# Output-weight preparation moved ahead beside the feature-map folding, its stores issued later, and the last block's quotients multiplied on VectorE

## The chip, the cores and the metric

One core of one Trainium2 chip runs the whole kernel. The metric is the device time of one execution in microseconds (us), as a median over several runs. The work is done by TensorE (PE; its weight loads are shown as PEld), VectorE (DVE), ScalarE (ACT) and GpSimd (POOL), and SyncE (SP) issues nearly all transfers from one queue, in order.

## What is computed

```python
x  = A_x                                   # 1 x 2048 x 640
xn = layernorm(x)                          # over the 640 columns
# A: linear attention, 32 heads of 20, with a learned feature map w_phi per head
q, k, v = xn_A @ wqkv                      # 640 -> 3 * 640
phi(u)  = concat(softmax(u @ w_phi), softmax(-(u @ w_phi)))        # u = q or k, 40 features
kv, z   = phi(k)^T v, sum_s phi(k)
a = ((phi(q) kv) / (phi(q) z + 1e-6)) @ wo                         # 640 -> 640
# B: MLP, 640 -> 1728 -> 640
b = gelu(layernorm(xn) @ w1 + b1) @ w2 + b2
return x + a + b
```

`phi`'s products are folded into the weights: `wk` and `wq` are multiplied by `w_phi` once, so that keys and queries come out of one product as feature maps.

## The kernel before

All products run in float32r, with each operand split into a high and a low part (`hi`: a ScalarE copy with rounding, `lo`: the difference, one subtraction), and three matmuls per product (`mm3`, lines 70 to 72: hi by hi, hi by lo, lo by hi). The 2048 tokens are four blocks `b` of 512. The MLP's 14 chunks of 128 hidden units go in pairs `g`: `passes(g, b, ws)` makes the first layer of two chunks (PSUM bank, gelu on ScalarE at line 285, split at lines 61 and 64 into tiles `m`), and then the second layer, five banks of 128 outputs, each added by VectorE to `acc[b]` (lines 328 and 330). Three PSUM banks serve the second layer in turn, so TensorE can start a bank only when VectorE has read the one three before it.

Other work is laid beside the matmuls by hand. `Mlp.tick` is called after every group of three matmuls and advances the generator in `mlp.beside` by one step; whatever the generator emits stands at that place in each engine's program. TensorE's order is the written one throughout, and in the MLP and in the last parts of the kernel so are those of VectorE, ScalarE and GpSimd. An engine does its program in order, so an instruction that waits holds up all behind it; but an engine that waits for nobody runs ahead of the tick at which an instruction was written. SyncE's queue is ordered by a scheduler.

The places that matter here:

- `next_y`, beside pass (1, 0): y of block 1 is made from `acc1` and broadcast rows `m5`, for five chunks `c`: GpSimd subtracts (line 637), VectorE multiplies (639), ScalarE rounds (641), VectorE subtracts (643). The next pass's first matmuls read it.
- `prep`, beside the passes for blocks 0 and 1, from pass (1, 1) on. First seven jobs fold `w_phi` into `wk` and `wq` (`prep_fold`, matmuls at line 698, splits at 713 and 715). Then a list `events` of steps with tick numbers: the y of blocks 2 and 3, chunk by chunk (`load`, `centred` 769, `scaled` 772, `hi` 776, `lo` 780, and differences of them, `combine` 792 and `combined_lo` 797, stored to `y_dram` and `t_dram` from a tile `t` with two buffers), and among them `wo_steps(q)`, the output weights: load, four sums of quarter tiles on GpSimd (`add`, 817), `hi` on ScalarE (823), `lo` on GpSimd (827) with the store of both parts right behind it (829). The five chunks of `wo` make three groups `q`.
- `Attention.quotients`, for each block: after the denominators' round trip through memory, five shuffles on VectorE (1287) and five multiplications on GpSimd (1289) make `ob`.
- The output product at the end, for blocks 0 and 1 and then 2 and 3: `ob` is split (`plain`, line 1302) and combined (`combine`, 1475), the combinations are split (`turn`, 1302), and the banks are read by VectorE into the sum (1516). `plain` gives the `lo` of block 2 to GpSimd and that of the others to VectorE.

Of the kernel before, what the change touches and what calls it, by code (L numbers as in the profile page):

```python
# [8 lines left out]
F32 = mybir.dt.float32  # L9
F32R = mybir.dt.float32r  # L10
AF = mybir.ActivationFunctionType
ALU = mybir.AluOpType
# [3 lines left out]
P = 128  # L16
S, D, F, H, DH = 2048, 640, 1728, 32, 20
KC = D // P
# [28 lines left out]
def f(ap):  # L47
    return ap.bitcast(F32)
# [3 lines left out]
def tile_kernel(ctx: ExitStack, tc: tile.TileContext, x, xT, wkT, wqT, wv, wphi, wo, w1, b1, w2, b2,  # L52
                ident, mmask, emask, vsel, out):
    nc = tc.nc
# [35 lines left out]
    wo_dram = [tc.dram_tile([P, 2, 2048], F32, name=f"wo{p}") for p in "hl"]  # L90
    wo4_dram = [tc.dram_tile([P, D], F32, name=f"wo4{p}") for p in "hl"]
# [26 lines left out]
    rp = ys.enter_context(tc.tile_pool(name="raw", bufs=1))  # L118
    wp = ys.enter_context(tc.tile_pool(name="w", bufs=1))

    def mtile(i, dtype=F32):
        return mp.tile([P, 2, D if i < 5 else 512], dtype, name=f"m{i}")
    y = {}

    def load_x(ts, xp, tag="xb"):
        xbs = []
# [88 lines left out]
    class Mlp:  # L215
# [21 lines left out]
        def fetch(self, c, pool=None):  # L237

            for p in self.fetch_parts(c, pool):
                p()  # L240
# [275 lines left out]
    mlp = Mlp((0, 1, 2, 3), ((0, 2), (1, 3)))  # L516
# [51 lines left out]
    def step(gen, n):  # L568
        for _ in range(n):
            next(gen, None)  # L570
# [169 lines left out]
    def prep():  # L740
        jobs = [units[o:o + 2] for o in range(0, 14, 2)]
        ahead = raws(jobs[0])
        more = more_stats()
        for i, job in enumerate(jobs):
            for k, _ in enumerate(prep_fold(job, ahead)):
                if k == 0 and i < 6:
                    ahead = raws(jobs[i + 1])
                if i > 0 and k % 3 == 1:
                    next(more, None)
                yield  # L750

        for _ in more:
            yield
        mr = {2: load_rows(2), 3: load_rows(3, 6)}

        raw = fp.tile([P, D], F32, name="raw").rearrange("p (c d) -> p c d", c=KC)
        nc.sync.dma_start(raw, wv[:, VF * H:].rearrange("(c p) d -> p c d", p=P))
        for _ in range(8):
            yield
        split(*[w[:, :, C2:C3] for w in wkv_], raw)  # L760

        xs, hls, events = {}, {}, []

        def load(c, b):
            xs[c, b] = fp.tile([P, 512], F32, name="xq", bufs=4)
            nc.sync.dma_start(xs[c, b], xT[c * P:(c + 1) * P, b * 512:(b + 1) * 512])

        def centred(c, b):
            nc.gpsimd.tensor_tensor(xs[c, b], xs[c, b], mr[b][:, 0], op=ALU.subtract)  # L769

        def scaled(c, b):
            nc.vector.tensor_tensor(xs[c, b], xs[c, b], mr[b][:, 1], op=ALU.mult)

        def hi(*at):
            hls[at] = fp.tile([P, 2, KC, G5], F32R, name="t").rearrange("p a c f -> p a (c f)")[:, :, :512]
            nc.scalar.activation(hls[at][:, 0], xs[at], AF.Copy)

        def lo(*at):
            hl = hls.pop(at)
            nc.vector.tensor_tensor(hl[:, 1], xs[at], f(hl[:, 0]), op=ALU.subtract)  # L780
            for p in range(2):
                nc.sync.dma_start(y_dram[at[1] - 2][p][:, at[0], :], f(hl[:, p]))

        def combined(q, i):

            c0, c1 = 2 * q, 2 * q + 1
            return {0: ((c0, 2), (c0, 3), (c0, 2)), 2: ((c0, 3), (c1, 3), (c0, 3)),
                    1: ((c1, 3), (c1, 3), (c0, 2)), 3: ((c1, 2), (c1, 2), (c1, 3))}[i]

        def combine(q, i):  # L790
            out, x0, x1 = (xs[at] for at in combined(q, i))
            nc.gpsimd.tensor_tensor(out, x0, x1, op=ALU.subtract)

        def combined_lo(q, i):
            at = combined(q, i)[0]
            hl = hls.pop(at)
            nc.vector.tensor_tensor(hl[:, 1], xs[at], f(hl[:, 0]), op=ALU.subtract)
            nc.sync.dma_start(t_dram[q][:, i], f(hl))

        def wo_steps(q):  # L800

            chunks = range(2 * q, min(2 * q + 2, KC))
            raw = []

            def fetch():
                for c in chunks:
                    raw.append(fp.tile([P, D], F32, name="raw"))
                    nc.sync.dma_start(raw[-1], wo[c * P:(c + 1) * P, :])

            def add(i):  # L810
                if i == 0:
                    raw.append(rp.tile([P, 6 * P], F32, name="s"))
                sm = raw[2].rearrange("p (i k n) -> p i k n", i=3, k=2)
                (a11, a21), (a12, a22) = ([r[:, :512].rearrange("p (k j n) -> p j k n", k=2, j=2)[:, j] for j in range(2)] for r in raw[:2])
                o, x0, x1, op = ((sm[:, 0], a21, a22, ALU.add), (a21, a11, a21, ALU.subtract),
                                 (sm[:, 1], sm[:, 0], a11, ALU.subtract), (sm[:, 2], a12, sm[:, 1], ALU.subtract))[i]
                nc.gpsimd.tensor_tensor(o, x0, x1, op=op)  # L817

            his = {}

            def hi(n, o, w):
                his[n, o] = fp.tile([P, D], F32R, name="wpt", bufs=1)[:, :w]
                nc.scalar.activation(his[n, o], raw[n][:, o:o + w], AF.Copy)

            def lo(n, o, w):
                src = raw[n][:, o:o + w]
                nc.gpsimd.tensor_tensor(src.bitcast(F32R), src, f(his[n, o]), op=ALU.subtract)
                for p, x in enumerate((f(his[n, o]), src)):
                    nc.sync.dma_start(wo_dram[p][:, q, D * n + o:D * n + o + w] if q < 2 else wo4_dram[p], x)

            steps = [(0, fetch, ())]
            if q < 2:
                steps += [(10 + 2 * i, add, (i,)) for i in range(4)]
            for n, piece in enumerate([(0, 0, D), (1, 0, D), (2, 0, 384), (2, 384, 384)] if q < 2 else [(0, 0, D)]):
                steps += [(18 + 7 * n, hi, piece), (19 + 7 * n, lo, piece)]
            return steps

        for q in range(3):
            events += [(4 + 46 * q + after, 1000 + len(events), step, args) for after, step, args in wo_steps(q)]
        base = 8  # L840
        for q in range(3):
            tiles = [(c, b) for c in range(2 * q, min(2 * q + 2, KC)) for b in range(2, 4)]
            for n, at in enumerate(tiles):
                for after, step in ((-6, load), (0, centred), (3, scaled), (5, hi), (7, lo)):
                    events.append((base + 5 * n + after, len(events), step, at))
            base += 5 * len(tiles) + 5
            if q < 2:
                for n, i in enumerate((0, 2, 1, 3)):
                    for after, step in ((0, combine), (3, lambda q, i: hi(*combined(q, i)[0])), (5, combined_lo)):
                        events.append((base + 4 * n + after, len(events), step, (q, i)))  # L850
                base += 19
        tick = 0
        for at, _, step, args in sorted(events, key=lambda e: e[:2]):
            while tick < at:
                tick += 1
                yield
            step(*args)

    def load_v():

        raws = [fp.tile([P, 2, KC, G5], F32, name="t").rearrange("p a c f -> p (a c f)") for _ in range(2)]
        raws = [raw[:, o:o + VF * H] for raw in raws for o in (0, VF * H)] + [fp.tile([P, D], F32, name="raw")[:, :VF * H]]
        for kc, raw in enumerate(raws):
            nc.sync.dma_start(raw, wv[kc * P:(kc + 1) * P, :VF * H])
        return raws
# [6 lines left out]

    p01 = mlp.passes(0, 1, [wc[0], wc[1]])
    next(p01)
    mlp.beside = prep()
    p11 = mlp.passes(1, 1, [wc[2], wc[3]])
    next(p11)
    finish(p01)
# [307 lines left out]
    class Attention:  # L1186
# [72 lines left out]
        def quotients(self):  # L1259
# [25 lines left out]
            for c in range(KC + 1):  # L1285
                if c < KC:
                    nc.vector.stream_shuffle(rx[:, c, :], rx[:, c, :], SPREAD)
                if c:
                    nc.gpsimd.tensor_tensor(ob[:, c - 1, :], ob[:, c - 1, :], rx[:, c - 1, :], op=ALU.mult)
                    if self.b < 2:  # L1290
                        nc.sync.dma_start(ob_dram[self.b][:, c - 1], ob[:, c - 1])
                for i in range(3):
                    yield
# [41 lines left out]
    def first_split():  # L1335
        at[0].oh, at[0].ol = (yp.tile([P, KC, 512], F32R, name=f"y{p}0") for p in range(2))
        for c in range(KC + 1):
# [3 lines left out]
                at[0].split(c - 1, 1)  # L1341
            if c % 2:
                yield

    def both(*gens):
        for _ in zip_longest(*gens):
            yield

    wol, phs = [], []
    ep = rx = None  # L1350
# [114 lines left out]
        return [z[:, 2 * q + i] for z in (at[b0 + j].oh, at[b0 + j].ol)]  # L1465

    def plain(b, c, part):
        return lambda: at[b].split(c, part, eng=nc.gpsimd if b == 2 else nc.vector)

    def combine(b0, i, q):  # L1470

# [166 lines left out]
```

## Time and profile before

| | |
|---|---|
| median of 3 runs | 721.48 us (721.33 to 729.02) |
| profiled execution | 720.63 us, span 718.8 us |
| busy: PE, PEld, DVE | 701.6, 586.2, 530.3 us |
| busy: ACT, POOL | 353.9, 476.7 us |
| moved by DMA | 109.72 MB, mean 153 GB/s |
| granted TensorE clock | 1.0 |

The span is what the profiler sees from the first to the last instruction; the profiled execution's own time is 1.8 us longer. Tables by stage give, for each engine, busy us and the number of instructions in a stretch of the span, then clock, DMA share and GB/s. In the timeline a row is start, duration, engine, line and operation, and in brackets how long the engine stood idle before it and on whom it waited.

### The profile page before, as it was taken

To read this page: it belongs to the slowest core of one execution; us is meant where nothing else is said; L and a number is where in the kernel's file an instruction comes from. 1 tells how busy PE (TensorE), PEld (TensorE's weight loads), DVE (VectorE), ACT (ScalarE), POOL (GpSimd) and SP (SyncE) were. 2 spreads that over 40 slices of the span, in tenths; PEclk is the share of its full clock that TensorE was granted. 3 is DMA by queue.
4 is the path that set the end of the run, shared out by engine and by line. 5 is a ranking of instruction groups with operands and counts; after the bars stand their busy time and mean duration, and the time that the engine had idled before them with its cause. 6 is when DMAs were issued, how large, how long until landed. Compare 5 with 4: busy or idle time off the path is not lost.

```text
span 718.8 us, 9827 instructions
## 1 busy us (share of the span) xinstructions
PE 701.6 (98%) x3357; PEld 586.2 (82%) x3357; DVE 530.3 (74%) x839; ACT 353.9 (49%) x583; POOL 476.7 (66%) x401
## 2 busy tenths in 40 slices
PE   8989999989899999999999999999999999999998
PEld 7868888777778888888888888888888878888777
DVE  7776755868654788987978777748678786789873
ACT  6434454444442544444454445547677666661320
POOL 3521223788616777887878869658588987475991
PEclk9999999999999999999999999999999999999999
DMA  9813643597753003603600705984345558755212
GB/s 325 294 40 106 197 136 118 200 319 238 255 174 147 1 1 146 147 2 147 146 1 1 187 1 205 275 245 130 120 118 179 172 164 273 263 193 184 81 71 102
DMA packets 67753, 109.72 MB, mean 153 GB/s; under 512 B 7655, under 2 KB 33031, under 8 KB 66079
## 3 DMA queue, kind: packets, MB, share of 16 engines
q1 hardware_dynamic: 67398, 109.08, 47.4%
q8 instruction: 26, 0.43, 0.2%
q14 instruction: 25, 0.20, 0.1%
q10 hardware_dynamic: 304, 0.01, 0.0%
HBM read 72.95 MB, written 36.12 MB: 152 GB/s over the span
## 4 chain that ended last, share of the span: by engine, by line
PE 66%; POOL 11%; issue 8%; DVE 7%; DMA 5%; ACT 2%; SPq 0%; ACTq 0%; POOLq 0%; DVEq 0%
PE bank L940 28%; PE bank L70 10%; PE bank L71 10%; PE bank L72 10%; POOL w L64 2%; PE bank L1010 2%; DMA r<-in_w 2%; POOL xq L769 1%; PE bank L1238 1%; PE bank L1239 1%; POOL acc L1475 1%; POOL y L1302 1%; DVE acc L330 1%; POOL s L817 1%; POOL tf L1475 1%
## 5 line engine op out<-in xcount | busy, mean ns | idle before, releaser
L940 PE MATMUL bank<-wkh,y 128*128 128x512 f32 (+1 forms) x480 | 139.5, 364 | 0.0
L70 PE MATMUL bank<-m,w 128*128 128x512 f32 x280 | 110.8, 396 | 9.8 <-DVE acc L330 9.5
L64 POOL TENSOR_TENSOR w<-r,w 128x640 fp32r<-128x640 f32 x32 | 52.9, 1667 | 87.4 <-ACT w L61 56.5
L71 PE MATMUL bank<-m,w 128*128 128x512 f32 x280 | 109.1, 390 | 0.0
L72 PE MATMUL bank<-m,w 128*128 128x512 f32 x264 | 102.8, 390 | 0.0
L70 PE MATMUL bank<-y,w 128*128 128x512 f32 (+1 forms) x254 | 99.0, 390 | 0.5 <-ACT m L285 0.4
L940 PEld LDWEIGHTS bank<-wkh,y 128*128 128x128 f32 x480 | 87.5, 188 | 13.3
L71 PE MATMUL bank<-y,w 128*128 128x512 f32 (+1 forms) x254 | 98.2, 387 | 0.0
L72 PE MATMUL bank<-y,w 128*128 128x512 f32 (+1 forms) x228 | 88.4, 388 | 0.0
L940 PE MATMUL bank<-wkl,y 128*128 128x512 f32 (+1 forms) x240 | 87.4, 364 | 0.0
L70 PEld LDWEIGHTS bank<-m,w 128*128 128x128 f32 x280 | 52.6, 188 | 24.4 <-DVE acc L330 12.9
L976 ACT ACTIVATE m<-m,rs_all 128x1280 f32<-128x1280 f32 x32 | 43.6, 1364 | 39.3 <-POOL m L975 39.2
L71 PEld LDWEIGHTS bank<-m,w 128*128 128x128 f32 x280 | 52.6, 188 | 10.5 <-DVE m L460 0.2
L975 POOL TENSOR_TENSOR m<-m,mx 128x640 f32<-128x640 f32 (+2 forms) x48 | 44.5, 942 | 22.4 <-DVE mx L964 22.3
L72 PEld LDWEIGHTS bank<-m,w 128*128 128x128 f32 x264 | 49.5, 188 | 10.4
L978 DVE TENSOR_REDUCE sm<-m 128x64 f32<-128x1280 f32 x32 | 47.4, 1482 | 13.7 <-ACT m L976 13.6
L940 PE MATMUL bank<-w,y 128*128 128x512 f32 x240 | 57.4, 391 | 0.0
L70 PEld LDWEIGHTS bank<-y,w 128*128 128x128 f32 x254 | 47.7, 188 | 11.0 <-issue 0.6
L64 DVE TENSOR_TENSOR m<-m,m 128x512 fp32r<-128x512 f32 (+1 forms) x34 | 28.1, 832 | 37.9 <-ACT m L61 37.8
L71 PEld LDWEIGHTS bank<-y,w 128*128 128x128 f32 x254 | 47.7, 188 | 9.7 <-DMA y<-t 0.4
L330 DVE TENSOR_TENSOR acc<-bank,acc 128x512 f32<-128x512 f32 x70 | 46.6, 680 | 9.2 <-PE bank L326 4.6
L957 ACT ACTIVATE m<-bank 128x512 f32<-128x512 f32 (+3 forms) x64 | 26.2, 436 | 55.1 <-PE bank L940 48.3
(223 smaller groups left out, 1609.9 us busy)
## 6 DMA issues: line engine op xcount, KB each, us to landing
r<-in_w SPq DMA_DIRECT2D x52, 320.0 KB
e<-e SPq DMA_DIRECT2D x40, 256.0 KB
e<-acc SPq DMA_DIRECT2D x52, 160.0 KB
acc<-in_xT SPq DMA_DIRECT2D x4, 1280.0 KB
t<-t SPq DMA_DIRECT2D x8, 512.0 KB
tf<-t SPq DMA_DIRECT2D x2, 1536.0 KB
xb<-in_x SPq DMA_DIRECT2D x8, 320.0 KB
xq<-in_xT SPq DMA_DIRECT2D x10, 256.0 KB
```

What stands on the lines that cost most here:

```text
L64: eng.tensor_tensor(lo, src, f(hi), op=ALU.subtract)
L70: nc.tensor.matmul(ps, lh, rh, start=first, stop=False, **kw)
L71: nc.tensor.matmul(ps, lh, rl, start=False, stop=False, **kw)
L72: nc.tensor.matmul(ps, ll, rh, start=False, stop=last, **kw)
L330: nc.vector.tensor_tensor(acc[b][:, m, :], pw, acc[b][:, m, :], op=ALU.add)
L940: nc.tensor.matmul(ps, lh[:, kc, c], rh[:, kc], start=n == 0, stop=n == 3 * KC - 1)
L957: return nc.scalar.activation(p3[:, :, 1 + f0:1 + f0 + src.shape[2]], src, AF.Copy).ins
L975: subs[n, t] = nc.gpsimd.tensor_tensor(ep[:, s], a, b, op=ALU.subtract)
L976: exps[n, t] = nc.scalar.activation(e, e, AF.Exp, scale=rs_all[:, t:t + 1])
L978: nc.vector.tensor_reduce(sm, e.rearrange("p s (h f) -> p (s h) f", f=DH), axis=AX, op=ALU.add)
L1010: nc.tensor.matmul(kvp[g // 2][:, (g % 2) * 240:(g % 2) * 240 + 240].rearrange("p (s f) -> p s f", s=4), v[:, g * VS:(g + 1) * VS], ft[:, ...
L1475: return lambda: nc.gpsimd.tensor_tensor(at[b0 + bo].ob[:, co], at[b0 + bx].ob[:, cx], at[b0 + by].ob[:, cy], op=ALU.subtract)
```

## The change

Three things are done.

1. `wo_steps` goes, and a generator `wo_parts` of its own takes its place, run in step with `prep` from pass (1, 1) on (`mlp.beside = both(prep(), wo_parts())`). It has the same sums and splits, on the same engines, but at ticks 0 to 98 counted from the start of the folding, where the old list began only after it. Chunks are taken as 512 columns in the four buffers named `xq`, which the y of blocks 2 and 3 uses later, and the last 128 columns of all chunks as one tile.
2. The stores of a split are a step of their own, three ticks after `lo`.
3. In `quotients` the last block's (b = 3) five multiplications go to VectorE, and in `plain` the `lo` of block 2's chunks 3 and 4 too.

```diff
+    def wo_parts():
+
+        def tile512(dtype=F32):
+            return fp.tile([P, 512], dtype, name="xq", bufs=4)
...
+        def fetch(c):
+            raw[c] = tile512()
+            nc.sync.dma_start(raw[c], wo[c * P:(c + 1) * P, :512])
...
+        def add(q, i):
...
+            nc.gpsimd.tensor_tensor(o, x0, x1, op=op)
+
+        def piece(tick, n, o, w, dest):
+
+            def hi():
+                his[tick] = tile512(F32R)[:, :w]
+                nc.scalar.activation(his[tick], raw[n][:, o:o + w], AF.Copy)
+
+            def lo():
+                src = raw[n][:, o:o + w]
+                nc.gpsimd.tensor_tensor(src.bitcast(F32R), src, f(his[tick]), op=ALU.subtract)
+
+            def store():
+                for p, z in enumerate((f(his[tick]), raw[n][:, o:o + w])):
...
+                    nc.sync.dma_start(to, z)
+
+            steps.extend([(tick, hi), (tick + 1, lo), (tick + 4, store)])
+
+        for c, t in enumerate((0, 1, 27, 32, 67)):
+            steps.append((t, lambda c=c: fetch(c)))
+        steps.append((75, fetch_last))
+        for q in range(2):
+            steps += [((9, 42)[q] + 2 * i, lambda q=q, i=i: add(q, i)) for i in range(4)]
+            for n, (name, o, w, at) in enumerate(((2 * q, 0, 512, 0), (2 * q + 1, 0, 512, D), ("s", 0, 384, 2 * D), ("s", 384, 384, 2 * D + 384))):
+                piece((17, 50)[q] + 5 * n, name, o, w, lambda p, q=q, at=at, w=w: wo_dram[p][:, q, at:at + w])
+        piece(74, 4, 0, 512, lambda p: wo4_dram[p][:, :512])
+        for q in range(2):
+            piece(84 + 5 * q, "m", 256 * q, 256, lambda p, q=q: wo_dram[p][:, q, :2 * D].rearrange("p (r d) -> p r d", r=2)[:, :, 512:])
+        piece(94, "m", 512, P, lambda p: wo4_dram[p][:, 512:])
...
-    mlp.beside = prep()
+    mlp.beside = both(prep(), wo_parts())
...
-                    nc.gpsimd.tensor_tensor(ob[:, c - 1, :], ob[:, c - 1, :], rx[:, c - 1, :], op=ALU.mult)
+                    (nc.gpsimd if self.b < 3 else nc.vector).tensor_tensor(ob[:, c - 1, :], ob[:, c - 1, :], rx[:, c - 1, :], op=ALU.mult)
...
-        return lambda: at[b].split(c, part, eng=nc.gpsimd if b == 2 else nc.vector)
+        return lambda: at[b].split(c, part, eng=nc.gpsimd if b == 2 and c < 3 else nc.vector)
```

In the changed kernel the new lines are 845 (`add`), 851 (`hi`), 855 (`lo`), 862 (store) and 1314 (the multiplication); 637 became 641, 769 became 773, 1302 became 1327, 1287 became 1312, 1516 became 1537 and 1538 became 1559.

GpSimd's program around `next_y` (five subtractions into `xb`), before:

```order
L64 TENSOR_TENSOR w_177<-r_166,w_177 128x640
L637 TENSOR_TENSOR xb<-acc_106,m_412 128x512 x5
L64 TENSOR_TENSOR w_767<-r_563,w_767 128x640
L64 TENSOR_TENSOR w_767<-r_564,w_767 128x640
L64 TENSOR_TENSOR w_851<-r_772,w_851 128x640
```

and now:

```order
L64 TENSOR_TENSOR w_177<-r_166,w_177 128x640
L641 TENSOR_TENSOR xb<-acc_106,m_412 128x512 x5
L845 TENSOR_TENSOR s<-xq 128x256
L845 TENSOR_TENSOR xq<-xq 128x2x128
L845 TENSOR_TENSOR s<-s,xq 128x256
L845 TENSOR_TENSOR s<-xq,s 128x256
L855 TENSOR_TENSOR xq<-xq 128x512
L64 TENSOR_TENSOR w_779<-r_563,w_779 128x640
```

The first group's four sums and its first `lo` now stand directly behind the subtractions for y of block 1, where GpSimd's next work was the split of the next weights.

GpSimd's program in the second group of y tiles of blocks 2 and 3 (`xq`; the `w` rows are splits of MLP weights), before:

```order
L64 TENSOR_TENSOR w_1598<-r_1475,w_1598 128x640
L769 TENSOR_TENSOR xq<-xq,m_1176 128x512
L817 TENSOR_TENSOR raw<-raw 128x2x128
L817 TENSOR_TENSOR s<-s,raw 128x256
L817 TENSOR_TENSOR s<-raw,s 128x256
L769 TENSOR_TENSOR xq<-xq,m_1178 128x512
L827 TENSOR_TENSOR raw<-raw,wpt 128x640 x2
L792 TENSOR_TENSOR xq<-xq 128x512 x2
```

and now:

```order
L64 TENSOR_TENSOR w_1645<-r_1533,w_1645 128x640
L773 TENSOR_TENSOR xq<-xq,m_1236 128x512
L773 TENSOR_TENSOR xq<-xq,m_1238 128x512
L796 TENSOR_TENSOR xq<-xq 128x512 x2
L64 TENSOR_TENSOR w_1758<-r_1650,w_1758 128x640
```

All sums and splits of the output weights have left this stretch.

VectorE's program in the output product, from the fourth of the five shuffles of block 3 on (`rx` the quotients, `acc_5578` and `acc_5595` the `ob` of block 3, `bank` rows the reads that free PSUM for TensorE), before:

```order
L1287 STREAM_SHUFFLE rx<-rx 128x512
L1516 TENSOR_TENSOR w_6084<-bank_6092,w_6084 128x512
L1287 STREAM_SHUFFLE rx<-rx 128x512
L1516 TENSOR_TENSOR w_5972<-bank_6252,w_5972 128x512
L1516 TENSOR_TENSOR w_5972<-bank_6268,w_5972 128x512
L1516 TENSOR_TENSOR w_5972<-bank_6089,w_5972 128x512
L1302 TENSOR_TENSOR y_6087<-acc_5578,y_6086 128x512
```

and now:

```order
L1312 STREAM_SHUFFLE rx<-rx 128x512
L1314 TENSOR_TENSOR acc_5595<-acc_5595,rx 128x512
L1537 TENSOR_TENSOR w_6101<-bank_6109,w_6101 128x512
L1312 STREAM_SHUFFLE rx<-rx 128x512
L1314 TENSOR_TENSOR acc_5595<-acc_5595,rx 128x512
L1537 TENSOR_TENSOR w_5989<-bank_6269,w_5989 128x512
L1314 TENSOR_TENSOR acc_5595<-acc_5595,rx 128x512
L1537 TENSOR_TENSOR w_5989<-bank_6285,w_5989 128x512
L1327 TENSOR_TENSOR y_6052<-acc_5213,y_6051 128x512
L1537 TENSOR_TENSOR w_5989<-bank_6106,w_5989 128x512
L1327 TENSOR_TENSOR y_6052<-acc_5213,y_6051 128x512
L1327 TENSOR_TENSOR y_6104<-acc_5595,y_6103 128x512
```

Three of the five multiplications and the two splits of block 2 (`y_6052`) are seen among the reads of the banks; the other two multiplications stand earlier, one behind each shuffle from the second on.

More of the change, by code (lines that the diff above doesn't have):

```diff
@@ L123, in tile_kernel, with both @@
     y = {}
+    def both(*gens):
+        for _ in zip_longest(*gens):
+            yield
     def load_x(ts, xp, tag="xb"):
@@ L798, in combined_lo @@
             nc.sync.dma_start(t_dram[q][:, i], f(hl))
[L800 to L839, printed above, removed]
         base = 8
@@ L857, in prep, with fetch_last @@
             step(*args)
+    def wo_parts():
+        def tile512(dtype=F32):
+            return fp.tile([P, 512], dtype, name="xq", bufs=4)
+        raw, his, steps = {}, {}, []
+        def fetch(c):
+            raw[c] = tile512()
+            nc.sync.dma_start(raw[c], wo[c * P:(c + 1) * P, :512])
+        def fetch_last():
+            raw["m"] = rp.tile([P, 6 * P], F32, name="s")[:, :D]
+            nc.sync.dma_start(raw["m"].rearrange("p (c n) -> p c n", c=KC), wo[:, 512:].rearrange("(c p) n -> p c n", p=P))
+        def add(q, i):
+            if i == 0:
+                raw["s"] = rp.tile([P, 6 * P], F32, name="s")
+            sm = raw["s"].rearrange("p (i k n) -> p i k n", i=3, k=2)
+            (a11, a21), (a12, a22) = ([raw[2 * q + r].rearrange("p (k j n) -> p j k n", k=2, j=2)[:, j] for j in range(2)] for r in range(2))
+            o, x0, x1, op = ((sm[:, 0], a21, a22, ALU.add), (a21, a11, a21, ALU.subtract),
+                             (sm[:, 1], sm[:, 0], a11, ALU.subtract), (sm[:, 2], a12, sm[:, 1], ALU.subtract))[i]
+            nc.gpsimd.tensor_tensor(o, x0, x1, op=op)
[8 more added lines that the diff above has]
+                for p, z in enumerate((f(his[tick]), raw[n][:, o:o + w])):
+                    to = dest(p)
+                    if len(to.shape) > 2:
+                        z = z.rearrange("p (c n) -> p c n", n=P)
+                    nc.sync.dma_start(to, z)
[11 more added lines that the diff above has]
+        piece(94, "m", 512, P, lambda p: wo4_dram[p][:, 512:])
+        tick = 0
+        for at, step in sorted(steps, key=lambda e: e[0]):
+            while tick < at:
+                tick += 1
+                yield
+            step()
@@ L1343, in first_split @@
                 yield
-    def both(*gens):
-        for _ in zip_longest(*gens):
-            yield
     wol, phs = [], []
```

## The prediction, made before the changed kernel was run

> **What bounds the kernel now.** I read the busy shares first, then a table by stage, then TensorE's waits, and last the timeline around them.
>
> ```profile
> span 718.8 us, 9827 instructions
> PE 701.6 (98%) x3357; PEld 586.2 (82%) x3357; DVE 530.3 (74%) x839; ACT 353.9 (49%) x583; POOL 476.7 (66%) x401
> ```
>
> TensorE is busy for 701.6 of 718.8 us. The change leaves its program alone, so at most 17 us of idle time are to be won or added to. The stages (busy us and instructions of PE, PEld, DVE, ACT and POOL, then clock, DMA share, GB/s):
>
> ```profile
> 20.00:45.00 25.00, 22.56 (x98) 17.54 (x97) 20.79 (x39) 11.52 (x21) 14.12 (x9) 1.00 0.60 203
> 45.00:140.00 95.00, 94.84 (x474) 79.92 (x473) 62.02 (x119) 44.21 (x81) 30.79 (x21) 1.00 0.44 134
> 140.00:160.00 20.00, 17.00 (x74) 13.48 (x73) 12.09 (x16) 9.28 (x16) 16.62 (x12) 1.00 0.92 319
> 160.00:180.00 20.00, 18.39 (x81) 14.88 (x81) 16.68 (x20) 9.08 (x15) 17.16 (x13) 1.00 0.70 239
> 180.00:205.00 25.00, 22.41 (x98) 17.94 (x97) 16.05 (x25) 11.19 (x20) 11.61 (x9) 1.00 0.74 241
> 205.00:664.00 459.00, 458.02 (x2213) 387.00 (x2213) 352.27 (x528) 244.06 (x392) 340.54 (x304) 1.00 0.44 138
> 664.00:702.00 38.00, 36.89 (x159) 28.98 (x158) 29.05 (x44) 12.80 (x22) 38.00 (x28) 1.00 0.21 77
> ```
>
> Three stages matter: the y of blocks 2 and 3 with the output weights (140 to 205), where TensorE lacks 7.2 of 65 us; the start, beside `next_y`; and the output product from 664 on, where GpSimd is busy throughout. Beside the folding (45 to 140) TensorE lacks 0.2 us and GpSimd is busy for 31 of 95. The waits of PE from 140 to 205 and two of its restarts, with two matmuls of an unbroken run between them for measure:
>
> ```profile
> PE bank L70 <- DVE acc L330: 7.2, 5, 2.1
> ...
> 138.60 0.39 PE L70 MATMUL bank<-m,w 128*128 128x512 f32 x1
> 139.28 0.39 PE L70 MATMUL bank<-m,w 128*128 128x512 f32 x1
> ...
> 159.73 0.50 PE L70 MATMUL bank<-m,w 128*128 128x512 f32 x1 [2.06 <-DVE acc L330]
> 191.20 0.50 PE L70 MATMUL bank<-m,w 128*128 128x512 f32 x1 [2.07 <-DVE acc L330]
> ```
>
> Three matmuls take 0.68 us. Five times TensorE waits, 7.2 us in all, for VectorE's read of a bank (line 330), and each restart costs 0.50 − 0.39 = 0.11 more: 7.75 us.
>
> **Term 1: the middle, −7.4 us.** What holds VectorE there? First ScalarE's waits from 130 to 205, one of them in the timeline, and GpSimd's splits of the output weights from 130 to 210; then the timeline of the third stall:
>
> ```profile
> ACT t L776 <- DMA t<-t: 10.2, 3, 4.5
> 155.77 0.64 ACT L776 ACTIVATE t<-xq 128x512 fp32r<-128x512 f32 x1 [2.80 <-DMA t<-t]
> 130.00:210.00 80.00, 13.74 (x9) 1.00 0.77 260
> ...
> 165.45 1.74 POOL L769 TENSOR_TENSOR xq<-xq,m 128x512 f32<-128x512 f32 x1
> 167.15 0.74 POOL L817 TENSOR_TENSOR raw<-raw 128x256 f32<-128x256 f32 x1
> 171.86 1.56 POOL L827 TENSOR_TENSOR raw<-raw,wpt 128x640 fp32r<-128x640 f32 x1
> ...
> 171.93 2.04 DVE L772 TENSOR_TENSOR xq<-xq,m 128x512 f32<-128x512 f32 x1 [1.18 <-POOL xq L769]
> ```
>
> The third stall: between two subtractions (769) GpSimd makes sums of the output weights (817); VectorE's multiplication (772) waits 1.18 us for the second subtraction, then takes 2.04 us, because GpSimd began a split (827) 0.07 us earlier; the split ends at 173.42, the multiplication at 173.97, so its own work is 0.55. Behind it stand the split for the MLP and the read TensorE waits for. The second and fourth stalls begin on ScalarE: the rounding of a y chunk (776) waits for a tile `t` whose stores have not landed, and the MLP's gelu and rounding queue behind it. That is a stretch with a DMA share of 0.92, a third of whose traffic I estimate as the output weights' (6.5 MB of loads and stores in all by tile sizes, of about 18 MB that 140 to 205 moved by the GB/s column).
>
> After the change neither sums, splits nor transfers of the output weights are there. GpSimd loses 13.7 us of splits and some 4 to 8 us of sums out of 45, and the queue about a third of its load. I keep one short wait (0.35) for a multiplication that still meets a subtraction: −7.4. Ends: −7.75, all five go; −3.4, if the second and fourth (2.06 + 2.07 + 0.22 = 4.35) stay because the `t` stores land as late as now.
>
> **Beside the folding, nothing.** The work now lies in 45 to 140, about 14 + 8 us of GpSimd and nine roundings on ScalarE, where GpSimd stands idle for 64 of 95 us and ScalarE for 51; 6.5 MB over 95 us are 68 GB/s on top of 134. Stores three ticks later don't hold SyncE's queue, since what they wait for is then done. Were that cover gone, each fold split on VectorE could wait for one sum, up to 0.74, or one split, 1.56, behind matmuls with no spare time.
>
> **Term 2: the start, +1.5 us.** The first group's sums wait only for loads, and an engine that waits for nobody runs ahead of its tick. GpSimd's last subtractions and its next work, VectorE's queue then, TensorE's wait, and the DMA share after the start's loads:
>
> ```profile
> 26.00:28.00 2.00, 2.00 (x11) 1.65 (x10) 0.94 (x7) 1.45 (x3) 0.00 (x0) 1.00 0.16 57
> 35.37 5.09 POOL L637 TENSOR_TENSOR xb<-acc,m 128x512 f32<-128x512 f32 x3
> 68.25 3.07 POOL L64 TENSOR_TENSOR w<-r,w 128x640 fp32r<-128x640 f32 x2 [27.79 <-issue]
> 37.57 1.77 DVE L643 TENSOR_TENSOR y<-xb,y 128x512 fp32r<-128x512 f32 x1
> 39.86 1.15 DVE L639 TENSOR_TENSOR xb<-xb,m 128x512 f32<-128x512 f32 x1
> 40.94 0.68 DVE L643 TENSOR_TENSOR y<-xb,y 128x512 fp32r<-128x512 f32 x1
> 41.54 0.68 DVE L330 TENSOR_TENSOR acc<-bank,acc 128x512 f32<-128x512 f32 x1
> 42.27 0.50 PE L70 MATMUL bank<-m,w 128*128 128x512 f32 x1 [0.61 <-DVE acc L330]
> 45.74 0.68 DVE L643 TENSOR_TENSOR y<-xb,y 128x512 fp32r<-128x512 f32 x1
> 46.51 0.39 PE L70 MATMUL bank<-y,w 128*128 128x512 f32 x1
> ```
>
> Transfers are nearly done by 26, so the `wo` chunks are there. GpSimd ends its subtractions at 40.46 and was then free for 27.79 us; now four sums of 128x256 follow at once, against the VectorE work TensorE is already waiting for. The first sum waits for line 639 to end (41.01) and takes 0.74, to 41.75. Line 643 then ends at 41.75 + 0.55 = 42.30 instead of 41.62; the read behind it and TensorE are 0.68 late. The three other sums come between the later steps; followed through at 0.74 each, the last split (45.74, end 46.42) ends at 47.85. TensorE takes up the last chunk at 46.51 + 0.1, now 0.68 later, 47.3: 0.55 more. With two or three longer restarts (0.11 each) that is +1.5. Ends: 0, if VectorE always finds GpSimd between two sums; +3.1, if all four delay the chain (4 × 0.74 + 0.11).
>
> **Term 3: the end, +2.9 us.** VectorE in the output product, GpSimd beside it, TensorE's restarts, and PE's waits there:
>
> ```profile
> 673.66 0.69 DVE L1516 TENSOR_TENSOR w<-bank,w 128x512 f32<-128x512 f32 x1 [1.10 <-PE bank L72]
> 675.02 0.69 DVE L1516 TENSOR_TENSOR w<-bank,w 128x512 f32<-128x512 f32 x1 [0.67 <-PE bank L72]
> 675.63 1.28 DVE L1302 TENSOR_TENSOR y<-acc,y 128x512 fp32r<-128x512 f32 x1
> 680.46 1.37 DVE L1516 TENSOR_TENSOR w<-bank,w 128x512 f32<-128x512 f32 x2 [1.26 <-PE bank L72]
> ...
> 671.27 2.57 POOL L1302 TENSOR_TENSOR m<-tf,m 128x512 fp32r<-128x512 f32 x2
> ...
> PE bank L71 <- DVE e L1302: 0.6, 1, 0.6
> PE bank L71 <- POOL e L1302: 0.3, 1, 0.3
> PE bank L70 <- DVE w L1516: 0.2, 1, 0.2
> ```
>
> VectorE has 1.10 + 0.67 + 1.26 = 3.0 us to spare before its reads are late. Into this stretch go five multiplications and two splits, all with two inputs in SBUF, beside a GpSimd that is never idle. What one takes: 0.6 alone; 1.28 when GpSimd is met midway; 1.77 at the worst (the 37.57 row). I take one at 1.77, four at 1.25 and two, which follow one that has just waited, at 0.63: 8.0. One old split then waits 0.6 less, and 3.0 is to spare: the reads are 4.4 us late, and TensorE, whose banks wait for them, with them. Against it GpSimd's chain ends about 9 us sooner (seven instructions of 1.28, by the 671.27 row), so that the three waits, 1.1 us with 0.3 for restarts, go: 4.4 − 1.4, about +2.9. Ends: 7 × 0.6 − 0.6 − 3.0 − 1.4 = −0.8, and 7 × 1.77 − 5.0 = +7.4.
>
> [...]
>
> **The sum.** 1.5 − 7.4 + 2.9 = −3.0 us: the span 715.8, the profiled execution, 1.8 more, 717.6. It stood 0.85 under the median of 721.48, so the median becomes 718.5.
>
> **Rivals.**
>
> *The moved operations fall between GpSimd's.* Sums and multiplications meet no instruction: 0 − 7.4 − 0.8 = −8.2, 713.3 us. For it: several VectorE rows between 41 and 47 take 0.68. Against it: those are rows with GpSimd idle, and at the end it is never idle. Chance 0.17.
>
> *VectorE becomes the bound of the output product* (the slower side): each of the seven waits for a whole GpSimd instruction, +7.4; 1.5 − 7.4 + 7.4 = +1.5, 723.0 us. The change loses from the point where one added operation takes 1.56 us ((7.4 − 1.5 + 5.0) / 7). For it: VectorE can be caught again after each read; against it: the 1.28 row is the usual one there. Chance 0.15.
>
> *The middle doesn't come free.* `t` keeps two buffers and its stores, 512 KB each, remain; the second and fourth stalls stay: 1.5 − 3.4 + 2.9 = +1.0, 722.5 us. For it: three waits of 10.2 us on ScalarE are for just those stores; against it: a third of the transfers around them is gone. Chance 0.13.
>
> **How the numbers follow.** The forecast has 0.55. One per cent, 7.2 us, is about what a measurement of this kernel can tell from no change: faster needs under 714.3, which the first rival gives and the lower edge of the forecast touches (0.18); slower needs over 728.7, which only several upper ends together give (0.04); the rest is 0.78. The range goes from 712.8, the first rival with all five stalls gone and a little of the start's old wait, to 724.0, the second rival with one of the start's further sums.
>
> **What would show it.** In the changed profile: GpSimd's sums (845) from about 40.5 to 46, VectorE's 643 rows there over 1 us, and a PE stall near 42 and another before 49; no ScalarE wait on `t` stores and no PE stall over 0.4 us from 143 to 205; multiplications (1314) of 0.6 to 1.8 us and PE waiting for the banks' reads (1537) from 680 to 686 for about 4 us; no stall from 696 on. Wrong would be the sum if the PE waits of 140 to 205 remain above 3 us, if line 1314 takes 0.68 throughout, or if new waits appear between 45 and 140.

## The result, and the profile after

The changed kernel takes 720.65 us (median of 20 runs; 719.26 to 723.96), the kernel before 721.77 beside it (20 runs): a ratio of 0.9987, with a 95% interval of 0.9971 to 1.0003, which holds 1: no change can be told from none. Forecast were 718.5, 3.0 us less. A few executions take longer for a reason that stays open, among them four of e1's twelve below (724.41 to 729.66 us, at mean clocks of 0.988 to 0.993), one of e6's five (997.49) and one of e9's four (3691.61); the ratios leave out those over 1.5% above a kernel's fastest. The profiled execution took 721.94 us with a span of 720.1, 1.3 us more than before's. The page's head, as that of before:

```profile
span 720.1 us, 9864 instructions
PE 704.4 (98%) x3357; PEld 589.1 (82%) x3357; DVE 543.0 (75%) x846; ACT 354.3 (49%) x586; POOL 468.8 (65%) x397
```

TensorE is "busy" for 2.8 us more, with the same 3357 matmuls: some of them were slower. Four moments that both kernels have split the span: the 7th, 20th and 27th gelu of the MLP on ScalarE (line 285, now 289) and VectorE's last read of the MLP's banks (line 330, now 334). Their rows in the timelines, of before and then of the changed kernel:

```profile
47.45 0.69 ACT L285 ACTIVATE m<-bank,b1t 128x512 f32<-128x512 f32 x1 [2.16 <-PE bank L72]
140.83 0.67 ACT L285 ACTIVATE m<-bank,b1t 128x512 f32<-128x512 f32 x1
200.55 0.67 ACT L285 ACTIVATE m<-bank,b1t 128x512 f32<-128x512 f32 x1
652.89 0.62 DVE L330 TENSOR_TENSOR acc<-bank,acc 128x512 f32<-128x512 f32 x1
```

```profile
48.41 0.69 ACT L289 ACTIVATE m<-bank,b1t 128x512 f32<-128x512 f32 x1 [2.02 <-PE bank L72]
145.06 0.67 ACT L289 ACTIVATE m<-bank,b1t 128x512 f32<-128x512 f32 x1
197.42 0.67 ACT L289 ACTIVATE m<-bank,b1t 128x512 f32<-128x512 f32 x1
649.63 0.62 DVE L334 TENSOR_TENSOR acc<-bank,acc 128x512 f32<-128x512 f32 x1
```

Differences of these starts, with the span's end, give each stage's length in us (for the experiments in the same way):

| kernel | start | folding | middle | attention | end | span |
|---|---|---|---|---|---|---|
| before | 47.5 | 93.4 | 59.7 | 452.3 | 65.9 | 718.8 |
| changed | 48.4 | 96.7 | 52.4 | 452.2 | 70.5 | 720.1 |
| difference | +1.0 | +3.3 | −7.4 | −0.1 | +4.6 | +1.3 |
| forecast | +1.5 | 0 | −7.4 | 0 | +2.9 | −3.0 |

The middle first: PE's waits from 140 to 205, where five took 7.2 us before.

```profile
PE bank L70 <- DVE acc L334: 0.3, 1, 0.3
```

At the start GpSimd runs the four sums behind its subtractions, and VectorE's line 647 (643 before), 0.68 when left alone, takes 1.2 while it meets them; TensorE's second wait grows from 0.61 to 1.18:

```profile
40.44 1.19 POOL L845 TENSOR_TENSOR s<-xq 128x256 f32<-128x256 f32 x1
40.95 1.23 DVE L647 TENSOR_TENSOR y<-xb,y 128x512 fp32r<-128x512 f32 x1
42.83 0.50 PE L70 MATMUL bank<-m,w 128*128 128x512 f32 x1 [1.18 <-DVE acc L334]
43.30 1.22 DVE L647 TENSOR_TENSOR y<-xb,y 128x512 fp32r<-128x512 f32 x1
44.05 1.08 POOL L845 TENSOR_TENSOR s<-xq,s 128x256 f32<-128x256 f32 x1
```

Beside the folding a wait has appeared that the prediction has not. First before's stages from 75 to 95, then the changed kernel's, its TensorE rows and its clock by narrow stretches:

```profile
75.00:85.00 10.00, 10.00 (x54) 8.54 (x53) 8.08 (x20) 4.71 (x11) 3.12 (x2) 1.00 0.80 247
85.00:95.00 10.00, 10.00 (x55) 8.55 (x54) 5.24 (x19) 9.10 (x16) 3.10 (x2) 1.00 0.41 116
```

```profile
75.00:85.00 10.00, 10.00 (x54) 8.55 (x53) 7.09 (x17) 4.66 (x11) 4.17 (x3) 1.00 0.98 331
85.00:95.00 10.00, 8.09 (x36) 6.61 (x35) 7.15 (x21) 6.93 (x15) 5.96 (x6) 0.83 0.68 191
...
88.81 1.12 PE L702 MATMUL bank<-wpt,raw 120*128 120x114 f32 x8 [1.45 <-DMA raw<-in_wqT]
...
91.00:94.00 3.00, 3.00 (x11) 2.52 (x11) 2.29 (x8) 2.95 (x6) 2.92 (x4) 0.50 0.45 120
```

The DMA engines are full from 75 to 85 (share 0.98), a load for the folding lands late, TensorE waits 1.45 us (1.9 with a second wait), and behind that it runs at half its clock from about 90.8 to 94.2. New waits between 45 and 140 are what the prediction itself had named as a sign that it is wrong.

The end, by forms on VectorE from 660 to 690, PE's waits from 660 to 703, the two long ones, and the clock:

```profile
L1314 DVE TENSOR_TENSOR acc<-acc,rx 128x512 f32<-128x512 f32 x5 | 7.7, 1536 | 0.0
...
PE bank L70 <- DVE w L1537: 3.8, 3, 2.3
...
680.31 0.50 PE L70 MATMUL bank<-y,r 128*128 128x512 f32 x1 [0.84 <-DVE w L1537]
683.55 0.48 PE L70 MATMUL bank<-y,w 128*128 128x512 f32 x1 [2.29 <-DVE w L1537]
...
683.00:684.70 1.70, 1.15 (x5) 0.99 (x6) 1.70 (x4) 0.00 (x0) 0.57 (x2) 1.00 0.98 361
684.70:688.20 3.50, 3.50 (x10) 2.73 (x9) 3.50 (x4) 1.26 (x2) 2.81 (x3) 0.51 0.35 124
688.20:689.00 0.80, 0.80 (x5) 0.66 (x4) 0.80 (x1) 0.00 (x0) 0.80 (x1) 1.00 0.00 0
```

TensorE waits 3.8 us for VectorE's reads of the banks, where about 4 were forecast, and here too it is at half clock for 3.4 us afterwards. The median is lower than the profiled execution, and by the mean clocks both drops are not always there: of the 20 executions three have a mean clock of 1.0 and take 719.26 to 720.59, ten of 0.997 or 0.998 (room for one such stretch: half of 3.4 is 1.7, 0.24% of the span), 720.02 to 722.06, and seven of 0.994 or 0.995 (room for two), 721.94 to 723.96. The means of the three groups are 720.0, 720.7 and 722.7.

### The profile page after: what moved, and what is told of

The parts are those of the page before. It is cut to its first block, busy times and chain, and to the rows that moved or that the text cites. A ratio compares the mean times of both kernels' runs of the same rounds, so it can differ in the third digit from the quotient of the medians.

```text
span 720.1 us, 9864 instructions
## 1 busy us (share of the span) xinstructions
PE 704.4 (98%) x3357; PEld 589.1 (82%) x3357; DVE 543.0 (75%) x846; ACT 354.3 (49%) x586; POOL 468.8 (65%) x397
## 4 chain that ended last, share of the span: by engine, by line
PE 82%; DVE 8%; DMA 3%; issue 3%; POOL 2%; ACT 1%; SPq 0%; ACTq 0%; POOLq 0%; DVEq 0%
PE bank L965 27%; PE bank L70 15%; PE bank L71 15%; PE bank L72 15%; PE bank L1035 2%; PE bank L702 2%; DMA r<-in_w 1%; POOL w L64 1%; PE bank L1263 1%; PE bank L1264 1%; DVE w L1537 1%; DMA raw<-in_wqT 1%; DVE acc L334 1%; DVE y L1327 1%; DVE y L647 1%
## 5 line engine op out<-in xcount | busy, mean ns | idle before, releaser
L70 PEld LDWEIGHTS bank<-y,w 128*128 128x128 f32 x254 | 48.6, 191 | 13.2 <-issue 2.7
L1003 DVE TENSOR_REDUCE sm<-m 128x64 f32<-128x1280 f32 x32 | 47.4, 1482 | 13.8 <-ACT m L1001 13.6
L71 PEld LDWEIGHTS bank<-y,w 128*128 128x128 f32 x254 | 48.5, 191 | 10.2 <-DVE y L647 0.6
L64 DVE TENSOR_TENSOR m<-m,m 128x512 fp32r<-128x512 f32 (+1 forms) x34 | 26.3, 781 | 37.6 <-ACT m L61 37.5
L982 ACT ACTIVATE m<-bank 128x512 f32<-128x512 f32 (+3 forms) x64 | 26.2, 436 | 55.1 <-PE bank L965 48.4
```

Source lines behind the costliest of these rows:

```text
L64: eng.tensor_tensor(lo, src, f(hi), op=ALU.subtract)
L70: nc.tensor.matmul(ps, lh, rh, start=first, stop=False, **kw)
L71: nc.tensor.matmul(ps, lh, rl, start=False, stop=False, **kw)
L982: return nc.scalar.activation(p3[:, :, 1 + f0:1 + f0 + src.shape[2]], src, AF.Copy).ins
L1003: nc.vector.tensor_reduce(sm, e.rearrange("p s (h f) -> p (s h) f", f=DH), axis=AX, op=ALU.add)
```

## The experiments

The theory was that three losses, each in its own place, ate a middle that did what was forecast. Where a ratio stands, it is to the kernel before, with its 95% interval.

**The third part undone, and alone.** e1 in the changed kernel:

```diff
-(nc.gpsimd if self.b < 3 else nc.vector).tensor_tensor(ob[:, c - 1, :], ...)
+nc.gpsimd.tensor_tensor(ob[:, c - 1, :], ...)
-eng=nc.gpsimd if b == 2 and c < 3 else nc.vector
+eng=nc.gpsimd if b == 2 else nc.vector
```

> The changed kernel without its third part: the last block's quotients and block 2's splits are GpSimd's again. Theory (the seven operations make VectorE late for the banks of the output product, 2.8 us of stalls, and the stalls there pull the granted clock to half for 3.4 us, 1.6 more): PE waits less than 0.5 us in all for line 1537, the clock is 1.0 after 650, the small stalls near the very end come back (1.1 us), and the time is 1.5 to 3.5 us under the changed kernel's 720.65, so about 718. Rival (the end waits for GpSimd's chain, which then is 9 us longer; the third part was needed once the middle is faster): the gain at the banks is given back at the end, the time is 720.5 or more. If clock drops have nothing to do with stalls, one is seen in the output product here as well.

e2 is the same edit the other way round, in the kernel before.

> The kernel before with the third part alone. Theory (third part costs the same wherever the middle stands): multiplications of 1.2 to 1.8 us, PE waiting for the banks' reads (1516) about 3.8 us from 670 to 690, the clock at half for some 3.4 us in most executions, and the time 1.5 to 4.5 us over the kernel before. Rival (VectorE meets GpSimd in the output product only because the rest is early): the operations take about 0.7 and the time is that of before within 0.5 us or under it.

e1: 717.32 us, 0.9952 (0.9917 to 0.9988); e2: 725.69, 1.0057 (1.0045 to 1.0069). The end takes 66.0 us in e1 and 70.5 in e2, against 65.9 before and 70.5 changed: the third part costs 4.5 us of span wherever the middle stands. PE's waits from 660 to 703 in e1 are before's again, and in e2 those of the changed kernel:

```profile
PE bank L71 <- DVE e L1327: 0.6, 1, 0.6
PE bank L71 <- POOL e L1327: 0.3, 1, 0.3
PE bank L70 <- DVE w L1537: 0.2, 1, 0.2
...
PE bank L70 <- DVE w L1516: 3.8, 3, 2.3
```

In the two profiles the mean clock is 1.0 in e1, and 0.998 in e2, where it drops after the same stalls. Both times lie in their expected ranges, and the part of the theory held that the drop at the end follows the stalls at the end.

**Which half of the third part.** e6 keeps only block 2's two splits on VectorE, e7 only the five multiplications.

> The changed kernel with the quotients back on GpSimd, so that of the third part only block 2's two splits stay on VectorE. Theory (each operation costs what it waits for GpSimd, two of them fit into VectorE's 3.0 us to spare): PE's waits for line 1537 stay under 0.5 us, and the time is that of e1_without_part3 within 0.7, or up to 0.7 under it, since GpSimd's chain at the end is 2.6 us shorter: 716.6 to 718. Rival (any addition there costs): 719 or more.

> The changed kernel with block 2's splits back on GpSimd, so that of the third part only the five multiplications stay on VectorE. Theory (five operations of about 1.5 are 7.7 us against 3.0 to spare): PE waits for line 1537 for 2.5 to 4 us, a clock drop behind that in most executions, 719.5 to 721. Rival (the splits were the part that cost): the waits stay under 1 us, and the time is within 1 us of e1_without_part3.

e6: 715.76, 0.9910 (0.9894 to 0.9925); e7: 719.28, 0.9968 (0.9953 to 0.9983). The end takes 65.1 in e6 and 69.2 in e7. PE waits from 660 to 703, of e6 and then of e7:

```profile
PE bank L70 <- DVE w L1537: 0.9, 1, 0.9
```

```profile
PE bank L70 <- DVE w L1537: 2.6, 2, 2.0
```

Two splits cost one wait of 0.9 and take away the three that e1 has: the end is 0.9 us shorter than in e1. (The expected wait of under 0.5 was too low, and e6's time lies 0.8 under the forecast range.) The five multiplications were the loss; e7 is 0.2 under its forecast, with the wait as expected.

**The folding's crowd, moved later.** e3 puts what lies between ticks 24 and 66 ten ticks later:

```diff
-for c, t in enumerate((0, 1, 27, 32, 67)):
+for c, t in enumerate((0, 1, 37, 42, 67)):
-((9, 42)[q] + 2 * i, ...)
+((9, 52)[q] + 2 * i, ...)
-piece((17, 50)[q] + 5 * n, ...)
+piece((17, 60)[q] + 5 * n + 10 * (q == 0 and n > 0), ...)
```

> The changed kernel with the steps of the output weights from tick 24 to 66 (last three stores of the first group, loads of chunks 2 and 3, the second group) ten ticks later, so that they leave the stretch in which the folding's weights are loaded. Theory (stores and loads of the output weights fill the DMA engines from 75 to 86, share 0.98 where it was 0.80, so that a load for the folding lands 1.45 and 0.47 us late and the clock falls behind that): no PE wait for raw<-in_wqT, clock 1.0 to 140, and 1.5 to 3.3 us under the changed kernel, about 718.5. Rival A (the load waits for buffers or for its turn in the queue whatever the share): the wait stays over 1 us. Rival B (the crowd only moves with the steps): a wait for another load between 88 and 140, of 1 us or more.

725.90 us, 1.0060 (1.0044 to 1.0076): 5 us worse than the changed kernel, and rival B. The wait for `raw<-in_wqT` is gone. But the load of the last columns needs the one buffer `s`, which the second group, now later, still uses; ScalarE waits for it, in order, with the MLP's gelu behind, and TensorE for the read behind that:

```profile
128.53 0.42 ACT L851 ACTIVATE xq<-s 128x256 fp32r<-128x256 f32 x1 [8.20 <-DMA s<-in_wo]
135.06 0.79 PE L70 MATMUL bank<-m,w 128*128 128x512 f32 x1 [4.58 <-DVE acc L334]
```

**The start's sums on VectorE.** e4:

```diff
-nc.gpsimd.tensor_tensor(o, x0, x1, op=op)
+(nc.gpsimd if q else nc.vector).tensor_tensor(o, x0, x1, op=op)
```

> The changed kernel with the first group's four sums on VectorE, which stands in its written order and does them behind the y of block 1. Theory (GpSimd runs these sums ahead of their ticks, from 40.4 to 45.1, and VectorE's 647 rows wait for them): the 647 rows are 0.68, PE's wait near 42 is 0.6 and not 1.2, line 334 at 44.45 starts about 1.1 us sooner, and the time is about 1.0 us under the changed kernel. Rival (the start's delay comes from the loads of the output weights, not from the sums): 647 rows of 1.2 us stay and the time doesn't move.

720.82 us, 0.9984 (0.9969 to 0.9998): not the 1.0 us under the changed kernel that was expected, although the start is before's again (47.4). VectorE does the sums between 59 and 68, where it is busy for 7.4 of 9 us, and TensorE has a new wait at 69. The DMA engines are as full from 75 to 85 as in the changed kernel, and yet the load for the folding is waited for 0.2 us only:

```profile
42.25 0.50 PE L70 MATMUL bank<-m,w 128*128 128x512 f32 x1 [0.63 <-DVE acc L334]
69.16 0.47 PE L70 MATMUL bank<-m,w 128*128 128x512 f32 x1 [1.06 <-DVE acc L332]
...
75.00:85.00 10.00, 10.00 (x54) 8.55 (x53) 7.05 (x17) 3.63 (x9) 3.92 (x3) 1.00 1.00 331
...
PE bank L702 <- DMA raw<-in_wqT: 0.2, 1, 0.2
```

The reason for the start's loss is shown. Why the time does not follow is not: in the profiled execution start and folding are 1.0 and 1.2 us shorter than in the changed kernel, in spite of the new wait, and the middle, the attention and the end 0.8, 1.0 and 1.2 longer, the end with 6.8 us at half clock instead of 3.4 (the mean clock is 0.995).

**The first group early.** e5 is e1 with e4's edit and

```diff
-for c, t in enumerate((0, 1, 27, 32, 67)):
+for c, t in enumerate((0, 1, 18, 20, 67)):
-((9, 42)[q] + 2 * i, ...)
+((1, 42)[q] + (1, 2)[q] * i, ...)
-piece((17, 50)[q] + 5 * n, ...)
+piece((5, 50)[q] + (3, 5)[q] * n, ...)
```

> The changed kernel without its third part (as e1_without_part3), and with the first group of output weights early: its sums on VectorE at ticks 1 to 4, its splits from tick 5 in steps of three, its stores at ticks 9 to 18, the loads of chunks 2 and 3 at 18 and 20. The stretch from 45 to 65, with a DMA share of 0.06 to 0.27, takes the transfers that stood at 75 to 86. Theory (the three losses are separate, and each is removed): no PE wait for raw<-in_wqT, PE's wait near 42 is 0.6, no wait over 0.5 for line 1537, clock 1.0, and about 715.0 us, 6.5 under the kernel before. Rival (a new wait for every one removed, as with e3's load of the last columns): a PE stall of over 1 us between 47 and 75 or 100 and 140, and 717 us or more.

713.27 us, 0.9881 (0.9865 to 0.9897), 1.7 under the expected 715.0. The start takes 47.4 and the folding 93.4 us, both as before the change; no wait for `raw<-in_wqT` is left. The transfers have gone where there was room (45 to 65 had a share of 0.17 in the changed kernel):

```profile
45.00:65.00 20.00, 20.00 (x106) 17.08 (x105) 12.58 (x23) 11.10 (x20) 4.53 (x4) 1.00 0.34 108
65.00:75.00 10.00, 9.77 (x52) 8.07 (x51) 9.18 (x20) 3.27 (x4) 3.07 (x2) 1.00 0.91 301
75.00:85.00 10.00, 10.00 (x54) 8.54 (x53) 7.94 (x20) 4.71 (x11) 3.12 (x2) 1.00 0.83 249
```

**Both.** e9 is e5 with e6's two splits.

> e5_early_group with block 2's two splits on VectorE, as in e6_splits_on_vector. Theory (start and folding from e5, end from e6, nothing shared between them): one PE wait of about 0.9 for line 1537, no stall in the last 10 us, no wait for raw<-in_wqT, and 1.0 to 1.6 us under e5_early_group, about 711.9. Rival (the end's gain in e6 was between-run scatter): within 0.5 of e5's 713.3.

712.15 us, 0.9868 (0.9853 to 0.9882): 1.1 us under e5, as expected, 9.4 under the kernel before, and 8.5 under the changed one's 720.65. e11 is the same kernel once more, for a profile of an execution near the median.

> The kernel of e9_early_and_splits once more, for its profile. From e5 and e6: PE's waits for line 334 under 4.2 in all, one of about 0.9 for line 1537, none for raw<-in_wqT, 1327 or 1316 rows at the end, clock 1.0, span about 710.3.

One execution, 713.17 us, span 711.4 where about 710.3 was expected, clock 1.0: start 47.3, folding 92.3, middle 53.2, attention 453.5, end 65.1. PE's waits, those above 0.8 us:

```profile
PE bank L70 <- DVE acc L334: 2.7, 3, 1.7
PE bank L581 <- POOL m L579: 1.3, 1, 1.3
PE bank L186 <- DVE xb L177: 1.0, 2, 0.6
PE bank L71 <- DVE m L464: 0.9, 1, 0.9
PE bank L70 <- DVE w L1537: 0.9, 1, 0.9
```

**The second part alone.** e10 is e6 with the stores back in the step of the split, `(tick + 1, store)` for `(tick + 4, store)`.

> e6_splits_on_vector with the second part of the change undone: the stores of a split of the output weights are issued in the step of the split again, and not three ticks later. Theory (beside the folding a store that waits in SyncE's queue for its split has nothing urgent behind it): the time of e6 within 0.7. Rival (the later stores are what keeps the folding's loads on time): PE's waits for raw<-in_wqT grow from 1.4 to over 2.5, a clock drop follows, 717.5 or more.

715.26 us, 0.9920 (0.9903 to 0.9936), e6 within 0.5: issuing the stores later did nothing that can be measured. (Its wait for `raw<-in_wqT` is 1.3, e6's 1.4.)

**What the middle's gain was.** e8, in the kernel before:

```diff
-nc.gpsimd.tensor_tensor(src.bitcast(F32R), src, f(his[n, o]), op=ALU.subtract)
+nc.gpsimd.tensor_tensor(src[:, :8].bitcast(F32R), src[:, :8], f(his[n, o])[:, :8], op=ALU.subtract)
```

> The kernel before, with GpSimd's splits of the output weights (line 827) made on 8 of their 384 or 640 columns; the low parts of the other columns are left out, all transfers stay. It asks what of the middle's 7.4 us was GpSimd's splits. Theory of the prediction (the second and fourth stalls come from the t stores landing late, under a DMA share of 0.92; the third from GpSimd): the second and fourth stall, 2.06 and 2.07 before, stay over 1.5 each, ScalarE still waits over 6 us for t<-t; the third and first shrink to under 0.7 each; about 2 to 3 us under the kernel before. Rival (GpSimd's work delays the whole chain, the transfers too, and the stores land in time once it is gone): all five stalls together under 3 us, and 5 us or more under the kernel before.

717.45 us, 0.9935 (0.9915 to 0.9954). PE's waits from 136 to 206 and ScalarE's for `t` from 130 to 205 in e8:

```profile
PE bank L70 <- DVE acc L330: 2.2, 3, 1.0
...
ACT t L776 <- DMA t<-t: 3.7, 2, 2.1
...
153.39 0.63 ACT L776 ACTIVATE t<-xq 128x512 fp32r<-128x512 f32 x1 [2.11 <-DMA t<-t]
157.35 0.50 PE L70 MATMUL bank<-m,w 128*128 128x512 f32 x1 [1.04 <-DVE acc L330]
```

All transfers were still there, and the DMA engines even fuller (a share of 0.97 from 140 to 160, 0.92 before); yet the stalls fall from 7.2 to 2.2 us, and ScalarE's waits for the landed stores from 10.2 to 3.7. The time, 4.4 us less, lies between the two expectations (up to 3, and 5 or more); the place decides for the rival in the main. The fourth stall, 2.07, is gone, and of the second, 2.06, half is left: 1.04, still behind a wait for a landing.

## Why the prediction was right or wrong

*The middle* was right in size: −7.4 forecast, −7.4 measured, waits of 7.2 to 0.3. Its reason for the second and fourth stall was wrong. I took them for transfers, because ScalarE waits for a landing there. By e8 the stores landed late mostly because they were issued late: the first store of the differences goes out at 144.64 there, at 147.46 before, and with the splits shortened 5.0 us of waits go, the transfers kept. Whether GpSimd held up the work that fills `t`, or the output weights' stores ahead in SyncE's queue, e8 does not separate. The number came out all the same, by luck, because the change takes away the splits and the transfers together. The rival that these stalls might stay rested on the same misreading. (The stretch moved 17.2 MB by the three rows, not about 18.)

*The start* was right, +1.0 for +1.5. The first row went as walked (647 ends at 42.18, 42.30 forecast); of the three further sums one delayed a VectorE operation, so that the last split ended 1.1 us later than before and not 1.4 as walked.

*The end*: the mechanism was right, the price was short by the clock. The five multiplications took 7.7 us, where the sum has 6.8 for the five that wait; the two splits took 0.7 each, where it has 0.63 for the two that don't, but because GpSimd, with less to do, stood idle from 676.1 to 679.8. TensorE's start-to-start times (0.23 for a matmul in an unbroken run) give 5.2 us of stalls and restarts after 660, forecast 4.4, against 2.3 before, of which I had counted 1.4. The difference, +2.9, is the forecast one, but by luck: both terms were too small by about as much. The other 1.7 are the 3.4 us at half clock (0.50 from 684.75 to 688.15). The rival that the moved operations fall between GpSimd's is out, since each multiplication took 1.2 to 1.8. That VectorE becomes the bound was the forecast in small, not a rival beside it. Where I summed seven operations, e6 and e7 show that two are worth it and five are not: a sum for each half would have been the better account.

*Beside the folding, nothing*: this step failed, by 3.3 us in the profiled execution. In e1, e6 and e10, whose crowd is nearly the same but whose mean clock is 1.0, the folding is 1.1 to 1.5 longer than before. I added 68 GB/s to a mean of 134 over 95 us, and a mean share of 0.44 says nothing of the ten microseconds from 75 to 85, which stood at 0.80 before. There the stores and loads of the output weights filled the engines (0.98), and a load that TensorE needs came late: some 2.1 us of waits and restarts, and the rest, about 1.2, by the clock (0.50 from 90.8 to 94.2). e3 and e5 show it: with the crowd moved the wait is gone, and in e5 the first group's transfers some 20 us earlier cost nothing. How late the load comes beside the same crowd varies: TensorE's waits for it were 1.9 in the changed kernel, 1.6, 1.4 and 1.3 in e1, e6 and e10, and 0.2 in e4, so in these runs the full stretch (a share of 0.98, in e4 of 1.00) took away the load's margin and didn't fix the price.

*What the sum did not have at all* are the stretches at half clock behind TensorE's stalls, 3.4 us twice. In this execution they made 1.7 + 1.2 of the 4.3 us between the forecast span and the measured one; 2.1 more came from the folding's waits, and the start gave 0.5 back. In the median, with room for one drop rather than two, the miss is 2.1 us. But a low mean clock is not a price by itself. Of 20 executions of the kernel before that ran beside e1 and took 720.2 to 723.3 us, 14 show 0.997 to 0.999; in the mean they took 721.6, the six at 1.0 721.5. In the changed kernel's profile the last matmul ends at 716.9, and from 718.9 to the end, with no matmul left to slow, the clock is at half again (0.50). Had such a drop begun with the last matmul, 3.2 us at half would make 0.998 by themselves. So how much of the median is due to drops stays open; the 1.7 and 1.2 hold for the profiled execution.

## What to carry to other kernels

Work that is moved into idle time has to be checked against the fullest ten microseconds of its new place and not against the stage's mean; here the same transfers cost 1.1 to 3.3 us at one place and nothing some 20 us earlier. An engine that waits for landed stores may only be showing that they were issued late (with the first store issued 2.8 us sooner, ScalarE's waits fell from 10.2 to 3.7 us in e8), so shorten the producer before the transfers are blamed. The five multiplications, with two inputs in SBUF, cost VectorE 1.54 us each here while GpSimd was busy for 12.0 of 12 us (664 to 676), where the two splits took 0.68 with GpSimd idle; such operations are worth moving only as long as the spare time of the reads behind them holds: two were, five were not.

## What the runs showed of the hardware

In some executions the granted clock was at half for 3.4 us, or twice that, behind waits of TensorE. In the changed kernel 0.84 and 2.29 us of idle time within some 4 us were followed by 3.4 us at 0.50 (684.75 to 688.15), and waits of 1.45 and 0.47 by 3.4 us at 0.50 (90.8 to 94.2); 4.58 in one piece (e3) was followed by 6.8 us at half (the mean clock of that execution is 0.993). One wait of 2.06 us between full stretches (159.73, before) was followed by none (1.00 from 157 to 165), and waits of 1.6 and 1.4 in all for the folding's load (e1 and e6) by none (a mean clock of 1.0 in both). So nearly the same stalls were followed by a drop in some executions only; how much idle time it takes, and what else decides, was not measured by itself.
